# Projections in 64-row pairs, one step of maxima inside every tile, and the maxima turned in the middle of a burst

## The chip, the cores and the metric

The kernel runs on one core of a Trainium2 chip. The metric is device time in microseconds (us) of one launch. The kernel before the change takes 1880.69 us, the median of 3 runs (1880.5 to 1881.56).

A core has a matrix engine (TensorE, in the profile PE, with its weight loads listed apart as PEld), a vector engine (VectorE, DVE), a scalar engine (ScalarE, ACT), a general engine (GpSimd, POOL) and an engine that here only issues transfers (SyncE, SP). Matrix products are written to PSUM, 8 banks of 128 partitions by 512 words; everything else lives in SBUF or in DRAM.

## What is computed

The reference, cut to what matters (S = 2048 rows, D = 640 columns, H = 32 heads of 20):

```python
g = sigmoid((x * gate_w).sum(-1))
qkv = x @ wqkv
scores = einsum("bhqd,bhkd->bhqk", q, k) * 20 ** -0.5
a = softmax(scores) @ v, heads joined, @ wo
re, im = x @ dft_hid_re.T, x @ dft_hid_im.T   # the same x
b = dft_seq_re @ re - dft_seq_im @ im
out = g * a + (1 - g) * b
```

The wqkv and wo inputs are scaled up, so the softmax needs true row maxima, and the kernel splits its matrix operands into two parts (a rounded one and the rest) and adds three products of parts.

## The kernel before

**Stages.** First q, k and v are projected and part of the hidden-dimension DFT is made (to about 255 us of the profile). Then follows the attention, 32 units of one head pair by one half of the rows. Each unit has 32 steps. With it run the rest of the hidden DFT, the sequence DFT and the output projection, as filling work on PE. A short tail writes the last rows.

**Projection stage.** `qk_tile(c, t)` (L302) makes one 128 x 512 tile of q or k: for 5 blocks of D it issues three products of parts (`three`, L118 to L121) into one bank, each with 128 contraction rows, so 15 matmuls. ACT copies the bank into half of a `p` tile (L320), POOL splits the copy into two parts (L115, L116, from `split`), and SP stores it to `qk_scr` (L300, from `flush`). The loop at L438 runs 32 such tiles. Before every third of them `segment` (L378) runs one tile of the hidden DFT. `hid_tile` (L353) works in pairs: every product is cut into two halves of 64 contraction rows, on the upper and lower half of the array, each half with its own bank (`yp0`, `yp1`), 15 pairs of 320 columns; ACT copies one bank and DVE adds the other (L371, L372). Between the pairs `segment` issues four steps of maxima, at the places that FILL gives (0, 8 and 7 pairs apart).

**A step of maxima** (`s_step`, L189, and `s_mm`, L161): two matmuls of 60 contraction rows by 512 columns, one per head of the pair and so one per half of the array, and for each a DVE reduction of the bank to row maxima (L173). These score tiles are made twice: once query-major for the maxima (kind "m" in ORDER), later key-major for the exponential (kind "e", L880, exp on ACT at L886). The maxima run ahead of the exponentials by LEAD = 41 steps. The first 41 are made in the projection stage: 40 in the ten segments, one by `run_s(LEAD)` after the last tile.

**Cycles of the attention.** A cycle is four steps in the order that ORDER writes out: 8 e, 8 m, fillings (F), and at its end B, the burst: `burst(c)` (L892) finishes maxima (`max_nm`, L185), reads out filling work, and runs two `av_step`s (L527): probabilities times values, 128 rows by 21 columns, on four column quarters of the array at a time.

**The turn of the maxima** (`max_chain`, L202). When all 32 steps of a unit have their maxima, `max_nm` reduces them to 128 x 16 (L187). At the end of that burst PE turns the 16 columns into rows (a transpose against `ident`, L205) in a bank of the rotation, DVE splits the result in two parts (16 x 128), and two steps later SP copies them in four transfers (L213, L214) into rows 60 and 61 of each head's block in `qst`. The e-scores have 62 contraction rows: the two extra ones subtract the maxima. So the first e-score of a unit waits for these transfers.

**Banks.** `bank()` (L125) hands out `ps0` to `ps4` in turn; `av`, `yp0` and `yp1` are the other three. SP issues its transfers in program order, and `at_step(i, fn)` places what a function issues at the beginning of step i.

**Weights.** `load_wqk` (L269) is issued after tile t = 1 of a group of four and split there one group later, on ACT and DVE (`fin()`).

Of the kernel before, what the change touches and what calls it, by code (L numbers as in the profile page):

```python
# [11 lines left out]
R = mybir.dt.float32r  # L12
# [28 lines left out]
LEAD = 41  # L41


FILL = {4: (0, 8, 7, 0)}
# [31 lines left out]
def mix_kernel(ctx: ExitStack, tc: tile.TileContext, xa, wqk, wb, cdft, wo, out):  # L76
# [21 lines left out]
    o_scr = dram.tile([D, S], F32, name="o_scr")  # L98

# [23 lines left out]
    turn = itertools.count()  # L123

    def bank():  # L125
        return ps_w.tile([P, 512], F32, name=f"ps{next(turn) % 5}")
# [48 lines left out]
    def s_end(i):  # L175
# [6 lines left out]
        if s == 1 and 0 < n <= NU and now[0] < 0:  # L182
            max_chain(n - 1)

    def max_nm(n):  # L185
        nms[n] = small.tile([P, 16], F32, name="nm", bufs=2)
        dve.tensor_reduce(nms[n], mx.pop(n).rearrange("p h q c -> p (h q) c"), axis=AX.X, op=ALU.max, negate=True)  # L187
# [14 lines left out]
    def max_chain(n):  # L202
        q = q_unit(n)
        pt = bank()[:16, :P]
        pe.transpose(pt, nms.pop(n), ident)  # L205
        m1 = small.tile([16, P], R, name="m1")
        m2 = small.tile([16, P], R, name="m2")
        split(m1, m2, pt, dve, dve)

        def rows():  # L210
            for h in range(2):
                b = 64 * h + KROWS
                sp.dma_start(f32(q[b : b + 1, :]), f32(m1[8 * h : 8 * h + 8, :]))  # L213
                sp.dma_start(f32(q[b + 1 : b + 2, :]), f32(m2[8 * h : 8 * h + 8, :]))  # L214

        if now[0] < 0:
            rows()
        else:
            at_step(now[0] + 2, rows)
# [82 lines left out]
    def qk_tile(c, t):  # L302
        w = wt[c]
# [11 lines left out]
        if hid_done:  # L315
            if not halves:
                raw = pair_tile()
                halves.extend((raw[:, 1], raw[:, 0]))
            raw = halves.pop()
            act.activation(raw, ps, AF.Copy)  # L320
        st = pair_tile()
        st1, st2 = st[:, 0].bitcast(R), st[:, 1].bitcast(R)
        if hid_done:
            split(st1, st2, raw, pool, pool)
        else:
            split(st1, st2, ps, act, dve)
        stores.append((qk_scr[:, t, c * P : (c + 1) * P].rearrange("z p c -> p z c"), st))
        flush(1 if hid_done else 2)
# [24 lines left out]
    def hid_tile(i, read_out):  # L353
        j, st = divmod(i, NS)
        hf, ri = divmod(j, 2)
        new_y(0), new_y(1)
# [21 lines left out]
    def segment(i, steps):  # L378
# [4 lines left out]
        tile_ = hid_tile(i, read_out)  # L383
        for n in FILL[steps]:
            run_s(step + 1)
            for _ in range(n):
                next(tile_)
# [40 lines left out]
    for s in range(0, NS, 2):  # L428
# [6 lines left out]
        if s == 12:  # L435
            fin()
            fin = load_wb(3)
# [606 lines left out]
```

## Time and profile before

| | |
|---|---|
| median of 3 runs | 1880.69 us (1880.5 to 1881.56) |
| the profiled execution's own time | 1881.58 us |
| its span | 1879.7 us |
| DVE busy in the span | 1446.3 us (77%) |
| ACT busy | 1224.5 us (65%) |
| POOL busy | 1075.1 us (57%) |
| granted TensorE clock | 1.00 in nearly every stretch |

Times in the views count from the start of the span. A row of the timeline has the start, the time from the first start to the last end of the merged instructions, the engine, the line, the operation, its tiles and shapes, and their number; in square brackets the idle time of the engine before it and what ended it. Matmuls are pipelined and their ends are modelled, so what a matmul costs is read from the distance between starts, not from its length. The row of a stretch has its length, then for PE, PEld, DVE, ACT and POOL the busy time and the number of instructions, the granted clock, the share of the DMA engines and GB/s.

### The profile page before, as it was taken

The numbers are of one execution on the slowest core, as the hardware profiler recorded it, in microseconds if no ns is written. First come the engines' busy times: TensorE is split into PE (matmuls) and PEld (weight loads), VectorE is DVE, ScalarE is ACT, GpSimd is POOL, SyncE is SP. The second block draws the span as 40 slices with busy tenths as digits, with TensorE's granted clock in tenths as the row PEclk, the third lists the DMA queues.
The fourth block names the chain that finished last, engine by engine and source line by source line (L and its number), as shares of the span: only waits on it lengthen the run. The fifth ranks groups of instructions, "written<-read, shape, count | busy, mean of one in ns | idle before, by whom it ended". The sixth has DMA issues, their size and how long they took to land. (4 is left out here: it accounts for less than half of the span.)

```text
span 1879.7 us, 44556 instructions
## 1 busy us (share of the span) xinstructions
PE 1870.3 (99%) x17453; PEld 1355.1 (72%) x17453; DVE 1446.3 (77%) x2404; ACT 1224.5 (65%) x2359; POOL 1075.1 (57%) x942
## 2 busy tenths in 40 slices
PE   9999999999999999999999999999999999999998
PEld 8988777777776767767677776776767777676666
DVE  4143469989898888888888888888888888889953
ACT  4221147777777767767676676766767667677785
POOL 1234421010045896566799899778789988634334
PEclk9999999999999999999999999999999999999999
DMA  7843341312325473536566576546476746342214
GB/s 233 180 137 141 134 140 48 80 59 66 115 69 185 147 230 125 162 123 189 194 182 226 173 241 197 167 131 188 162 234 197 213 152 202 112 111 68 62 36 159
DMA packets 174597, 280.51 MB, mean 149 GB/s; under 512 B 44095, under 2 KB 106687, under 8 KB 174387
## 3 DMA queue, kind: packets, MB, share of 16 engines
q1 hardware_dynamic: 173427, 275.69, 48.1%
q0 software_dynamic: 960, 1.97, 0.6%
q8 instruction: 137, 2.24, 0.5%
q14 instruction: 73, 0.60, 0.1%
HBM read 213.37 MB, written 63.52 MB: 147 GB/s over the span
## 5 line engine op out<-in xcount | busy, mean ns | idle before, releaser
L173 DVE TENSOR_REDUCE mx<-ps 128x1 f32<-128x512 f32 x2048 | 1296.1, 684 | 219.6 <-PE ps L171 199.6
L886 ACT ACTIVATE p<-ps 128x512 f32<-128x512 f32 x2048 | 1087.9, 598 | 429.3 <-PE ps L171 228.7
L171 PE MATMUL ps<-kst,qst 60*128 60x512 f32 x2048 | 776.5, 413 | 1.5 <-DVE mx L173 1.4
L880 PE MATMUL ps<-qst,kst 62*128 62x512 f32 x2048 | 698.4, 414 | 0.1
L614 PE MATMUL yp<-x,part 64*128 64x320 f32 x5376 | 645.8, 307 | 0.0
L614 PEld LDWEIGHTS yp<-x,part 64*128 64x128 f32 x5376 | 580.7, 186 | 7.2
L533 PE MATMUL av<-p,v 128*21 128x512 f32 x4096 | 490.6, 596 | 0.0
L880 PEld LDWEIGHTS ps<-qst,kst 62*128 62x128 f32 x2048 | 334.8, 184 | 202.5 <-DVE mx L173 182.2
L171 PEld LDWEIGHTS ps<-kst,qst 60*128 60x128 f32 x2048 | 368.2, 184 | 15.0 <-issue 3.8
L116 POOL TENSOR_TENSOR part<-raw,part 128x1024 fp32r<-128x1024 f32 (+1 forms) x129 | 290.3, 2251 | 10.3
L533 PEld LDWEIGHTS av<-p,v 128*21 128x21 f32 x4096 | 98.1, 100 | 225.8 <-issue 225.1
L363 PE MATMUL yp<-wb,x 64*128 64x320 f32 x1920 | 227.7, 307 | 0.3 <-ACT raw L371 0.2
L115 POOL CAST part<-raw 128x1024 fp32r<-128x1024 f32 (+1 forms) x129 | 127.1, 985 | 166.6 <-PE yp L614 155.3
L363 PEld LDWEIGHTS yp<-wb,x 64*128 64x128 f32 x1920 | 202.4, 186 | 5.2 <-DVE raw L372 0.8
L494 POOL TENSOR_TENSOR raw<-raw,raw 128x1024 f32<-128x1024 f32 x77 | 185.5, 2410 | 24.6 <-DMA raw<-in_cdft 23.7
L563 POOL TENSOR_TENSOR o<-o,rb 128x512 f32<-128x512 f32 x31 | 40.2, 1296 | 145.8 <-DMA rb<-r_scr 94.5
L119 PE MATMUL ps<-x,part 128*128 128x512 f32 (+1 forms) x236 | 90.7, 384 | 0.3
L685 PE MATMUL yp<-x,part 64*128 64x320 f32 x720 | 90.9, 310 | 0.0
L121 PE MATMUL ps<-x,part 128*128 128x512 f32 (+1 forms) x236 | 89.6, 380 | 0.1
L120 PE MATMUL ps<-x,part 128*128 128x512 f32 (+1 forms) x236 | 89.1, 377 | 0.0
L116 POOL TENSOR_TENSOR x<-araw,x 128x320 fp32r<-128x320 f32 x96 | 83.8, 873 | 7.7
L320 ACT ACTIVATE p<-ps 128x512 f32<-128x512 f32 x32 | 19.1, 598 | 93.8 <-PE ps L121 93.8
(85 smaller groups left out, 1142.2 us busy)
## 6 DMA issues: line engine op xcount, KB each, us to landing
raw<-in_cdft SPq DMA_DIRECT2D x192, 512.0 KB
araw<-a_scr SPq DMA_DIRECT2D x176, 160.0 KB
qk_scr<-p SPq DMA_DIRECT2D x40, 512.0 KB
kst<-qk_scr SPq DMA_DIRECT2D x90, 160.0 KB
qst<-qk_scr SPq DMA_DIRECT2D x90, 160.0 KB
a_scr<-raw SPq DMA_DIRECT2D x64, 160.0 KB
yt<-y_scr SPq DMA_DIRECT2D x64, 160.0 KB
y_scr<-yt SPq DMA_DIRECT2D x64, 160.0 KB
```

The lines of the kernel that those rows point to most:

```text
L115: e1.tensor_copy(dst1, src)
L116: e2.tensor_tensor(dst2, src, f32(dst1), op=ALU.subtract)
L119: pe.matmul(ps, st1, mv1, start=first, stop=False)
L171: pe.matmul(ps, q[b : b + KROWS, qt * P : (qt + 1) * P], k[b : b + KROWS, kc * 512 : (kc + 1) * 512], start=True, stop=True)
L173: return lambda: dve.tensor_reduce(mx[n][:, h, qt, kc : kc + 1], ps, axis=AX.X, op=ALU.max)
L363: pe.matmul(yp[h][:, :HE], xs[xz][t][r, d, cs], w[r, wz, d, :HE], start=d == 0 and z == 0, stop=d == ND - 1 and z == 2)
L494: pool.tensor_tensor(raws[0], raws[0], raws[1], op=ALU.add if PRODUCTS[n][0][1][0] > 0 else ALU.subtract)
L533: pe.matmul(av[32 * j : 32 * j + DH + 1, :], v[:, kt, h * (DH + 1) : (h + 1) * (DH + 1)], pp[qc][:, h, :], start=kt == 0, stop=kt == NS - 1)
L614: pe.matmul(yp[h][:, :HE], c[r, cz, cs], a[r, az], start=s == 0 and z == 0, stop=s == NS - 1 and z == 2)
L685: pe.matmul(yp[h][:, :HE], o[r, oz, d], wos[d, hf][r, wz], start=d == 0 and z == 0, stop=d == ND - 2 and z == 2)
L880: pe.matmul(pt, k[b : b + KROWS + 2, kt * P : (kt + 1) * P], q[b : b + KROWS + 2, qc * 512 : (qc + 1) * 512], start=True, stop=True)
L886: act.activation(pts[n, kt, qc][:, h], pt, AF.Exp, scale=float(DH) ** -0.5)
```

## The change

LEAD goes from 41 to 43. The projection tiles of the loop at L438 are made as the hidden DFT's are: each of the 15 products is a pair of 64-row matmuls into two banks, `ps0`/`ps1` and `yp0`/`yp1` by turns; ACT copies one bank, DVE adds the other, POOL splits as before. One step of maxima is issued after the seventh pair of every tile, hidden DFT or projection: 42 in 42 tiles, one more behind the last. While this stage runs, the maxima rotate through `ps2` to `ps4` only.

The turn of the maxima moves from the end of the burst in which they are finished to the middle of the next one, between its two `av_step`s. It is no longer one transpose but four plain matmuls, one for each quarter of 32 columns of `ident`, with the 16 columns of maxima doubled to 32, so that each fills one of the four column quarters of the array; the result is 128 x 32. DVE splits that, SP stores both parts to DRAM (`m_scr`, one transfer) one step later, and two steps after that loads them back from there into the rows of `qst` (four transfers, in pieces of 32 words).

```diff
--- before.py
+++ after.py
@@ -38,10 +38,10 @@
 FIRST = {"e": (0, 0, 1, 1), "m": (1, 1, 1, 1)}
 
 
-LEAD = 41
-
-
-FILL = {4: (0, 8, 7, 0)}
+LEAD = 43
+
+
+MARKS = (7,)
 HEAD = 10
 
 
@@ -96,6 +96,7 @@
     r_scr = dram.tile([NU, 4, 512], F32, name="r_scr")
     l_scr = dram.tile([NU, 4, 512], F32, name="l_scr")
     o_scr = dram.tile([D, S], F32, name="o_scr")
+    m_scr = dram.tile([NU, P, 2, 32], F32, name="m_scr")
 
     ident = const.tile([P, P], F32, name="ident")
     make_identity(nc, ident)
@@ -120,10 +121,15 @@
         pe.matmul(ps, st1, mv2, start=False, stop=False)
         pe.matmul(ps, st2, mv1, start=False, stop=last)
 
-    turn = itertools.count()
+    turn, twos, free = itertools.count(), itertools.count(), [range(5)]
 
     def bank():
-        return ps_w.tile([P, 512], F32, name=f"ps{next(turn) % 5}")
+        return ps_w.tile([P, 512], F32, name=f"ps{free[0][next(turn) % len(free[0])]}")
+
+    def two_banks():
+        if next(twos) % 2:
+            return [ps_w.tile([P, 512], F32, name=f"ps{z}") for z in range(2)]
+        return [ps_y.tile([P, 512], F32, name=f"yp{z}") for z in range(2)]
 
     def pair_tile():
         return work.tile([P, 2, 512], F32, name="p", bufs=5)
@@ -180,11 +186,12 @@
             else:
                 ends.append(n)
         if s == 1 and 0 < n <= NU and now[0] < 0:
-            max_chain(n - 1)
+            turn_max(n - 1)
 
     def max_nm(n):
-        nms[n] = small.tile([P, 16], F32, name="nm", bufs=2)
-        dve.tensor_reduce(nms[n], mx.pop(n).rearrange("p h q c -> p (h q) c"), axis=AX.X, op=ALU.max, negate=True)
+        nms[n] = small.tile([P, 32], F32, name="nm", bufs=2)
+        m = mx.pop(n).rearrange("p h q (o c) -> p o (h q) c", o=1).to_broadcast([P, 2, 16, 4])
+        dve.tensor_reduce(nms[n].rearrange("p (o k) -> p o k", o=2), m, axis=AX.X, op=ALU.max, negate=True)
 
     def s_step(i):
         for fn in [s_mm(i, h) for h in range(2)]:
@@ -199,24 +206,32 @@
         return yp[z]
 
 
-    def max_chain(n):
+    def turn_max(n):
         q = q_unit(n)
-        pt = bank()[:16, :P]
-        pe.transpose(pt, nms.pop(n), ident)
-        m1 = small.tile([16, P], R, name="m1")
-        m2 = small.tile([16, P], R, name="m2")
-        split(m1, m2, pt, dve, dve)
-
-        def rows():
+        pt = bank()[:, :32]
+        nm = nms.pop(n)
+        for j in range(4):
+            c = slice(32 * j, 32 * j + 32)
+            pe.matmul(pt[c, :], nm, ident[:, c], start=True, stop=True)
+        m = small.tile([P, 2, 32], R, name="m")
+        split(m[:, 0], m[:, 1], pt, dve, dve)
+
+        def store():
+            sp.dma_start(m_scr[n], f32(m))
+
+        def load():
             for h in range(2):
-                b = 64 * h + KROWS
-                sp.dma_start(f32(q[b : b + 1, :]), f32(m1[8 * h : 8 * h + 8, :]))
-                sp.dma_start(f32(q[b + 1 : b + 2, :]), f32(m2[8 * h : 8 * h + 8, :]))
+                for z in range(2):
+                    b = 64 * h + KROWS + z
+                    sp.dma_start(f32(q[b : b + 1, :]).rearrange("o (k j c) -> o k j c", j=4, c=32),
+                                 m_scr[n, :, z].rearrange("(o j k) c -> o k j c", o=1, j=4)[:, 8 * h : 8 * h + 8])
 
         if now[0] < 0:
-            rows()
+            store()
+            load()
         else:
-            at_step(now[0] + 2, rows)
+            at_step(now[0] + 1, store)
+            at_step(now[0] + 3, load)
 
 
     pa = pools(name="att", bufs=1)
@@ -300,6 +315,8 @@
             sp.dma_start(*stores.pop(0))
 
     def qk_tile(c, t):
+        if hid_done:
+            return qk_pairs(c, t)
         w = wt[c]
         ps = bank()
         x1, x2 = xs[0][t], xs[1][t]
@@ -312,20 +329,36 @@
                 pe.matmul(ps, w[:, 0, d], x2[:, d], start=False, stop=d == ND - 1)
             else:
                 three(ps, w[:, 0, d], w[:, 1, d], x1[:, d], x2[:, d], d == 0, d == ND - 1)
-        if hid_done:
-            if not halves:
-                raw = pair_tile()
-                halves.extend((raw[:, 1], raw[:, 0]))
-            raw = halves.pop()
-            act.activation(raw, ps, AF.Copy)
         st = pair_tile()
-        st1, st2 = st[:, 0].bitcast(R), st[:, 1].bitcast(R)
-        if hid_done:
-            split(st1, st2, raw, pool, pool)
-        else:
-            split(st1, st2, ps, act, dve)
+        split(st[:, 0].bitcast(R), st[:, 1].bitcast(R), ps, act, dve)
+        store_qk(c, t, st, 2)
+
+    def store_qk(c, t, st, keep):
         stores.append((qk_scr[:, t, c * P : (c + 1) * P].rearrange("z p c -> p z c"), st))
-        flush(1 if hid_done else 2)
+        flush(keep)
+
+    def tick(pairs):
+        if pairs in MARKS:
+            run_s(min(step + 1, LEAD))
+
+    def qk_pairs(c, t):
+        w = wt[c]
+        ps = two_banks()
+        for d in range(ND):
+            for z, (wz, xz) in enumerate(((0, 0), (0, 1), (1, 0))):
+                for h in range(2):
+                    r = slice(64 * h, 64 * h + 64)
+                    pe.matmul(ps[h], w[r, wz, d], xs[xz][t][r, d], start=d == 0 and z == 0, stop=d == ND - 1 and z == 2)
+                tick(3 * d + z + 1)
+        if not halves:
+            raw = pair_tile()
+            halves.extend((raw[:, 1], raw[:, 0]))
+        raw = halves.pop()
+        act.activation(raw, ps[0], AF.Copy)
+        dve.tensor_tensor(raw, raw, ps[1], op=ALU.add)
+        st = pair_tile()
+        split(st[:, 0].bitcast(R), st[:, 1].bitcast(R), raw, pool, pool)
+        store_qk(c, t, st, 1)
 
     def mm_b(j, s, ps, n):
         w = wt["b", j]
@@ -353,7 +386,7 @@
     def hid_tile(i, read_out):
         j, st = divmod(i, NS)
         hf, ri = divmod(j, 2)
-        new_y(0), new_y(1)
+        yp[:] = two_banks() if i < HEAD else [new_y(0), new_y(1)]
         w = wt["b", 2 + j]
         t, cs = st // 4, slice(st % 4 * P, (st % 4 + 1) * P)
         for d in range(ND):
@@ -375,16 +408,13 @@
         yield
 
 
-    def segment(i, steps):
+    def hid_first(i):
         def read_out(read, args):
             read()
             stores.append(args)
 
-        tile_ = hid_tile(i, read_out)
-        for n in FILL[steps]:
-            run_s(step + 1)
-            for _ in range(n):
-                next(tile_)
+        for pairs, _ in enumerate(hid_tile(i, read_out)):
+            tick(pairs + 1)
 
     step = 0
 
@@ -435,11 +465,12 @@
         if s == 12:
             fin()
             fin = load_wb(3)
+    free[0] = range(2, 5)
     for n, c in enumerate(order):
         for t in range(4):
             m = 4 * n + t
             if m % 3 == 0 and hid_done < HEAD:
-                segment(hid_done, 4)
+                hid_first(hid_done)
                 hid_done += 1
             qk_tile(c, t)
             if m == 8:
@@ -449,6 +480,7 @@
                     fin()
                 if n + 2 < len(order):
                     fin = load_wqk(order[n + 2])
+    free[0] = range(5)
     run_s(LEAD)
     flush()
 
@@ -889,16 +921,20 @@
 
             held.append(exp) if hold else exp()
 
+    turned = []
+
     def burst(c):
         for n in ends:
             max_nm(n)
         run_extras(max(done - HIDS, 0) // 3, 2)
         for kt in (2 * c, 2 * c + 1):
             av_step(now[0], kt // NS, kt % NS)
+            while turned:
+                turn_max(turned.pop(0))
             while held:
                 held.pop(0)()
-        while ends:
-            max_chain(ends.pop(0))
+        turned[:] = ends
+        ends.clear()
         if c == HID - 1:
             start_dft()
 
```

## The prediction

> **What bounds the kernel now.** I read the page first, then stretches of the span, then the order of time on single engines.
>
> ```profile
> PE 1870.3 (99%) x17453; PEld 1355.1 (72%) x17453; DVE 1446.3 (77%) x2404; ACT 1224.5 (65%) x2359; POOL 1075.1 (57%) x942
> L173 DVE TENSOR_REDUCE mx<-ps 128x1 f32<-128x512 f32 x2048 | 1296.1, 684 | 219.6 <-PE ps L171 199.6
> ```
>
> PE has work for the whole span, so whatever shortens the time must take something out of PE's stream: instructions, or gaps between their starts. DVE is the next engine (77%), nearly all of it reductions of maxima at 684 ns.
>
> The stretches: the projection stage, the first cycle of the attention, a cycle without and one with a turn of maxima, a late cycle with all 8 maxima and the last one that has any (4).
>
> ```profile
> 105.88:254.60 148.72, 147.20 (x862) 119.23 (x861) 60.99 (x101) 28.69 (x51) 62.63 (x62) 1.00 0.38 136
> 254.60:261.43 6.83, 6.65 (x54) 4.99 (x53) 6.29 (x11) 5.05 (x9) 1.90 (x2) 1.00 0.60 192
> 286.38:292.67 6.29, 6.29 (x64) 4.48 (x62) 5.56 (x10) 4.57 (x9) 0.00 (x0) 1.00 0.07 26
> 292.67:299.10 6.43, 6.43 (x65) 4.48 (x63) 6.12 (x13) 4.57 (x9) 0.00 (x0) 1.00 0.15 34
> 1790.12:1796.20 6.08, 6.08 (x58) 4.05 (x56) 5.54 (x10) 4.63 (x9) 3.23 (x4) 1.00 0.00 0
> 1802.38:1807.77 5.39, 5.39 (x53) 3.52 (x52) 4.63 (x10) 4.43 (x9) 3.09 (x4) 1.00 0.00 0
> ```
>
> In the projection stage DVE is busy 61 of 148.7 us, ACT 29, POOL 63: only PE can set its length. In a cycle DVE has 5.56 of 6.29 us: PE sets it, with some 0.7 us of room.
>
> PE in the projection stage, one segment, the five tiles behind it, and the two segments that stall:
>
> ```profile
> 233.88 0.73 PE L171 MATMUL ps<-kst,qst 60*128 60x512 f32 x4
> 234.44 1.34 PE L363 MATMUL yp<-wb,x 64*128 64x320 f32 x16
> 235.62 0.40 PE L171 MATMUL ps<-kst,qst 60*128 60x512 f32 x2
> 235.86 1.19 PE L363 MATMUL yp<-wb,x 64*128 64x320 f32 x14
> 236.89 0.40 PE L171 MATMUL ps<-kst,qst 60*128 60x512 f32 x2
> 237.22 0.50 PE L119 MATMUL ps<-x,part 128*128 128x512 f32 x1
> ...
> 254.28 0.40 PE L121 MATMUL ps<-x,part 128*128 128x512 f32 x1
> 254.60 0.50 PE L171 MATMUL ps<-kst,qst 60*128 60x512 f32 x2
> ```
>
> ```profile
> 133.79 0.72 PE L171 MATMUL ps<-kst,qst 60*128 60x512 f32 x4
> ...
> 136.63 0.50 PE L171 MATMUL ps<-kst,qst 60*128 60x512 f32 x1 [0.70 <-DVE mx L173]
> ...
> 138.43 0.50 PE L119 MATMUL ps<-x,part 128*128 128x512 f32 x1
> ```
>
> ```profile
> 193.36 0.50 PE L171 MATMUL ps<-kst,qst 60*128 60x512 f32 x1 [0.70 <-DVE mx L173]
> ```
>
> ```profile
> 135.15 0.82 DVE L116 TENSOR_TENSOR part<-raw,part 128x640 fp32r<-128x640 f32 x1 [9.14 <-ACT part L113]
> ```
>
> The 75 matmuls from 237.22 to 254.28 are 17.06 / 74 = 0.2305 us apart. Every change between 128-row and 64-row matmuls shows as a longer step: 0.32 instead of 0.23 at 254.28, 0.33 instead of 0.24 at 236.89. A plain segment takes 237.22 - 233.88 = 3.34 us; the one at 133.79 takes 4.64. There, four steps of maxima stand within 3 us, DVE came to them late because its queue held a split of weights (135.15), the banks were not free, and PE waited. The same happens at 193.36.
>
> **Pairs in the projections.** A pair does the work of one 128-row matmul, with twice the instructions. Its price is not in the trace for 512-wide projections, but its neighbours are: a step of maxima is a 512-wide pair, 0.24 us (235.62 to 235.86), and a 320-wide pair with the same 128-column weights takes 1.18 / 8 = 0.1475, so two weight loads fit even there. Lower bound the stream itself, 0.2305; upper bound 0.24. I take 0.2305: inside a run of pairs nothing changes width, and the matmul streams the same 512 columns.
>
> The stage after: 32 x 15 x 0.2305 = 110.6, 150 hidden pairs x 0.1475 = 22.1, 43 steps x 0.24 = 10.3 (two more than before), 0.1 for entering it and 0.3 for the first unit's turn: 143.4 against 148.72, **5.3 us less**. By parts that is ten times two changes of tile (about 0.2 us each time), the two stalls of 1.3, and less the two added steps (0.5). At 0.24 a pair the gain is 5.3 - 480 x 0.0095 = 0.7.
>
> What must stay hidden there: each tile adds a DVE addition, for which the nearest row is
>
> ```profile
> L116 DVE TENSOR_TENSOR p<-ps,p 128x512 fp32r<-128x512 f32 x8 | 5.3, 687 | 17.7 <-ACT p L113 17.7
> ```
>
> 0.69 us. With two reductions (1.37) DVE has 2.1 us of work in a tile of 15 x 0.2305 + 0.24 = 3.7 us, PE being the cover; POOL starts 0.7 later and has its slack in the first stretch above. A tile's banks are asked for again two tiles later, 3.7 us after its last matmul, against 0.6 + 0.69 us of read-out. Steps come 3.7 us apart on three banks, so the split of weights that stalled two segments delays two reductions and no longer PE. Cover gone (DVE late by more than a tile): 1.3 us each time, as seen.
>
> **The seam to the attention** loses. DVE sets the first cycle:
>
> ```profile
> 254.71 0.60 ACT L320 ACTIVATE p<-ps 128x512 f32<-128x512 f32 x1 [2.76 <-PE ps L121]
> ```
>
> ```profile
> 255.14 7.44 DVE L173 TENSOR_REDUCE mx<-ps 128x1 f32<-128x512 f32 x12 [15.46 <-PE ps L171]
> ```
>
> 6.29 of 6.83 us busy, twelve reductions without a gap, and PE waiting on banks. After the change the last tile's addition stands ahead of them in DVE's queue: ACT's copy ends 1.03 after the last matmul starts, the addition 0.69 later, so the reductions start at 1.72 instead of 255.14 - 254.28 = 0.86: **0.9 us more**. Bounds: 0 if later slack in DVE takes it up, 2 if the last `p` tiles, which POOL now finishes later, are waited for too.
>
> **The turn of the maxima.** PE and its weight loads in two bursts:
>
> ```profile
> 286.38 1.91 PE L533 MATMUL av<-p,v 128*21 128x512 f32 x16
> 288.23 0.50 PE L880 MATMUL ps<-qst,kst 62*128 62x512 f32 x1
> ```
>
> ```profile
> 292.67 1.92 PE L533 MATMUL av<-p,v 128*21 128x512 f32 x16
> 294.52 0.28 PE L205 MATMUL ps<-ident,nm 128*16 128x128 f32 x1
> 294.73 0.49 PE L880 MATMUL ps<-qst,kst 62*128 62x512 f32 x1
> ```
>
> ```profile
> 292.67 0.14 PEld L533 LDWEIGHTS av<-p,v 128*21 128x21 f32 x8 [0.24 <-issue]
> 293.12 0.12 PEld L533 LDWEIGHTS av<-p,v 128*21 128x21 f32 x4 [0.31 <-issue]
> 293.55 0.12 PEld L533 LDWEIGHTS av<-p,v 128*21 128x21 f32 x4 [0.31 <-issue]
> ```
>
> ```profile
> L205 PE MATMUL ps<-ident,nm x32: 276/277/278, 220.3 to 1809.6; 128*16 128x128 f32 x32
> ```
>
> The transpose makes the way from burst to next score 2.06 instead of 1.85 us: 0.21 each, in 31 bursts (the first turn is in the projections). In the middle of the burst the quarters use the array as the `av` products around them do: 128 rows, one column quarter each, four at a time. The rows show an fp32 product as two passes (16 records for two `av_step`s of 4), and a pass of 512 columns on four quarters takes 293.55 - 293.12 = 0.43 us. Two passes of 32 columns: 2 x 0.43 / 16 = 0.05. The weights of a pass of 128 columns in all load in the shadow of the pass ahead, except the second set, whose pass ahead is this short one; eight loads in 0.14 us put that at 0.02 or less. I take 0.07, a gain of 0.14 x 31 = **4.2 us**. Bounds: 0.05 (4.8 us), and, if PE drained ahead of and behind the quarters (0.1 each, as at the changes of tile above), 0.28, a loss of 2.2 us.
>
> The Trainium skill (TensorE: Matmul & The Clock Gate, Back-to-back issue gap) speaks against this part: however small its width, a matmul does not start sooner than about 25 ns after the one before. Eight such starts would by an estimate from that page take 0.2 us. The trace's weight loads, eight in 0.14 us, do not bear that out for neighbouring quarters.
>
> DVE's part stays about as it is (two splits of 0.28 at 16 x 128 now; smaller at 128 x 32; the reduction ahead of them reads twice as much), and falls into the burst, when DVE has its room. The turn uses one bank as before. SP gets five issues for four, one of which waits for another.
>
> **LEAD 43.** The two added steps are counted above. They fall out of the end: the cycle at 1802.38 loses its last 4 maxima. From 8 to 4 a cycle went from 6.08 to 5.39, 0.17 each; ACT has 4.43 us in it, so there is room: **0.5 us less** of the 0.69. The end of a unit's maxima moves one cycle forward, which leaves the turn in the cycle in which it is now.
>
> **Sum:** 5.3 - 0.9 + 4.2 + 0.5 = 9.1 us. The span would be 1879.7 - 9.1 = 1870.6; the profiled execution ran 1881.58, 0.05% above the median, so the same 9.1 come off the median: 1880.69 - 9.1 = **1871.6**.
>
> **Rivals.**
>
> *The rows of maxima come late (slower).* They now go by DRAM, and every unit's first e-scores wait for them.
>
> ```profile
> 295.14 0.66 SPq L213 DMA_DIRECT2D qst<-m  x1
> ...
> 297.27 0.64 SPq L214 DMA_DIRECT2D qst<-m  x1
> ```
>
> ```profile
> 304.97 0.46 PE L880 MATMUL ps<-qst,kst 62*128 62x512 f32 x2
> ```
>
> ```profile
> SPq L550 <- DMA l_scr<-o: 12.4, 12, 2.8
> ```
>
> ```profile
> 1819.20 1.28 POOL L563 TENSOR_TENSOR o<-o,rb 128x512 f32<-128x512 f32 x1 [0.86 <-DMA rb<-r_scr]
> ```
>
> ```profile
> 1813.93 1.75 SPq L560 DMA_DIRECT2D rb<-r_scr  x4
> ```
>
> From turn to need there are 304.97 - 294.52 = 10.45 us, and 0.86 more as the turn is two passes earlier. The chain at upper prices: 0.62 to the first issue, the store's issue 0.66 and its landing 2.8 (the longest wait of a load for a small store), four issues 297.91 - 295.14 = 2.8, a landing of 1819.20 - 1815.68 = 3.5: 10.4 of 11.3. Hidden by 0.9. It decides from there on: if SP's queue held store or loads 2 us longer (another transfer's wait between them), 30 units would each lose 1.1, 33 us, and the time be 1871.6 + 33 = 1905. For it: program order on SP, behind both. Against it: today's first issue follows the turn by 0.62.
>
> *The quarters cost what the transpose did*, by drains or by a floor on starts: 1871.6 + 4.2 = 1875.8.
>
> *512-wide pairs run at 0.24*, as a step of maxima between narrower pairs does: 1871.6 + 4.6 = 1876.2.
>
> *Both*, or one with the longer seam: about 1880, no change.
>
> **How the numbers follow.** Forecast (1869 to 1874) 0.60; quarters as dear as now 0.15; slow pairs 0.10; both, no change 0.07; rows late 0.08. From these, **1871.6**; the range 1867.5 to 1879 leaves out the late rows, most of the no-change case and a little below. A difference of 0.2% (3.8 us, about what a measurement of this kernel can tell from none) is 1876.9: faster 0.82, same 0.10, slower 0.08.
>
> **What would show it.** Pairs: projection matmuls of 64 rows 0.23 us apart, no step longer than 0.24 around the maxima, a stage of 143 us. Turn: burst starts to next score about 1.92 us in the cycle of a turn. Seam: the first reductions of the attention start 0.9 later. Rows: no wait of L880's weights for `qst` at the first score of a unit. Wrong it would be made by pairs over 0.24, by a wait there, or by a PE wait on banks in the projections.

## The result, and the profile after

The changed kernel takes 1871.3 us (median of 4, 1870.43 to 1871.84), the kernel before in the same session 1881.12 (median of 4): a ratio of 0.9947 with a 95% interval of 0.9935 to 0.9959. It is 9.8 us faster by the medians and 10.3 by the spans (1879.7 to 1869.4). The forecast was 1871.6.

The page of the kernel after, the busy time of the engines, the groups of the maxima and of the new projection pairs, and the queue of program fetches:

```profile
PE 1859.3 (99%) x18157; PEld 1356.1 (73%) x18157; DVE 1468.8 (79%) x2436; ACT 1223.4 (65%) x2359; POOL 1077.1 (58%) x942
...
q8 instruction: 143, 2.34, 0.5%
...
L179 DVE TENSOR_REDUCE mx<-ps 128x1 f32<-128x512 f32 x2048 | 1297.9, 684 | 200.0 <-PE ps L177 179.7
...
L351 PE MATMUL ps<-x,part 64*128 64x512 f32 x630 | 84.0, 390 | 0.0
```

PE still has work for the whole span, with more instructions than before; DVE has 22 us more, the additions of the pairs. ACT and POOL stay within 2 us of what they were. The stretches that answer to those of before: projection stage, first cycle, all cycles up to the last burst, tail.

```profile
105.90:249.79 143.89, 143.30 (x1353) 122.88 (x1354) 87.19 (x136) 28.71 (x51) 63.21 (x62) 1.00 0.39 141
249.79:257.33 7.54, 7.03 (x54) 4.88 (x50) 6.71 (x11) 4.96 (x9) 1.89 (x2) 1.00 0.53 172
257.33:1840.60 1583.27, 1583.27 (x16005) 1113.77 (x16004) 1331.27 (x2228) 1142.50 (x2203) 977.73 (x828) 1.00 0.50 147
1840.60:1869.40 28.80, 21.79 (x139) 18.46 (x138) 15.97 (x29) 9.52 (x18) 12.50 (x14) 0.95 0.53 197
```

The stage fell from 148.72 to 143.89 us, the first cycle rose from 6.83 to 7.54.

**The pairs.** PE in three projection tiles of the stage after:

```profile
235.08 1.77 PE L351 MATMUL yp<-x,part 64*128 64x512 f32 x14
236.68 0.41 PE L177 MATMUL ps<-kst,qst 60*128 60x512 f32 x2
236.92 2.01 PE L351 MATMUL yp<-x,part 64*128 64x512 f32 x16
238.76 1.77 PE L351 MATMUL ps<-x,part 64*128 64x512 f32 x14
240.36 0.40 PE L177 MATMUL ps<-kst,qst 60*128 60x512 f32 x2
```

Seven pairs take 240.36 - 238.76 = 1.60 us, eight take 238.76 - 236.92 = 1.84: 0.23 each, as forecast. The step of maxima between them takes 0.24. No distance between starts is longer here. Both stalls of before, 1.3 us each, are gone. One of 0.75 us has come up at another place, in the second hidden tile; PE, then DVE at the same place:

```profile
120.52 0.39 PE L177 MATMUL ps<-kst,qst 60*128 60x512 f32 x1
121.50 0.49 PE L177 MATMUL ps<-kst,qst 60*128 60x512 f32 x1 [0.59 <-DVE mx L179]
```

```profile
117.53 3.32 DVE L117 TENSOR_TENSOR wb<-raw,wb 128x966 fp32r<-128x966 f32 x2 [0.21 <-ACT wb L114]
120.77 1.27 DVE L179 TENSOR_REDUCE mx<-ps 128x1 f32<-128x512 f32 x2
```

The two halves of a weight block, split on DVE, last 3.3 us, nearly a whole tile (3.68 us, from 235.08 to 238.76), and hold up the reductions that free a bank. The kernel before made the same split at the same place, without a stall; there the maxima had five banks, not three:

```profile
117.94 2.88 DVE L116 TENSOR_TENSOR wb<-raw,wb 128x966 fp32r<-128x966 f32 x2 [6.26 <-ACT wb L113]
```

**The turn.** A burst with its turn, PE and then the weight loads:

```profile
288.49 1.06 PE L565 MATMUL av<-p,v 128*21 128x512 f32 x8
289.36 0.24 PE L215 MATMUL ps<-ident,nm 128*32 128x32 f32 x8
289.42 1.04 PE L565 MATMUL av<-p,v 128*21 128x512 f32 x8
290.39 0.50 PE L912 MATMUL ps<-qst,kst 62*128 62x512 f32 x1
```

```profile
288.93 0.13 PEld L215 LDWEIGHTS ps<-ident,nm 128*32 128x32 f32 x4 [0.31 <-DVE mx L179]
289.36 0.13 PEld L215 LDWEIGHTS ps<-ident,nm 128*32 128x32 f32 x4 [0.30 <-issue]
289.39 0.15 PEld L565 LDWEIGHTS av<-p,v 128*21 128x21 f32 x8
```

The eight records of the four quarters (two passes) take 289.42 - 289.36 = 0.06 us, and the `av` products ahead of them and behind them go on as if nothing stood between. Their weights load while the products before are still running (288.93); the load of the transpose, which started at 294.52 in the burst shown before, came only when its own turn had come:

```profile
294.51 0.09 PEld L205 LDWEIGHTS ps<-ident,nm 128*16 128x16 f32 x1 [0.85 <-DVE nm L187]
```

From burst to next score it is 290.39 - 288.49 = 1.90 us where it was 2.06.

**Where the 10.3 us come from.** Stage to its last projection matmul -4.7, from there to the first burst +0.6, from burst 0 to burst 244 -7.1, from 244 to 246 (the last maxima) -1.0, from the last burst to the end **+1.9**. The last was in no sum.

**The tail.** DMA in GB/s, in 40 slices of the time from the last burst to the end, before and after, and the SP issues of the last eight stores:

```profile
GB/s 365 15 0 0 0 0 0 259 228 0 0 255 339 381 400 354 241 61 65 61 61 388 423 176 0 148 385 419 415 183 396 362 358 366 411 419 404 122 0 0
```

```profile
GB/s 316 14 29 0 0 0 36 391 29 0 139 356 388 388 352 213 43 57 57 192 384 384 7 18 384 377 398 231 393 352 96 85 395 402 377 391 203 18 0 0
```

```profile
1869.84 6.13 SPq L954 DMA_DIRECT2D out_y<-x  x8
```

```profile
1857.64 7.05 SPq L990 DMA_DIRECT2D out_y<-x  x8
```

After, transfers fall to a quarter in the 31st and 32nd slice (96 and 85 GB/s, 21.6 to 23.0 us behind the last burst); before, the lowest slice in that part has 183. One of SP's eight issues, begun 20.96 us behind the last burst, took 1431 ns instead of 332. DVE finished its last rows 22.65 us behind the last burst in both: the work wasn't late, its stores were.

### The profile page after: what moved, and what is told of

It reads as the page before. It is cut to its first block, busy times and chain, and to the rows that moved or that the text cites. A ratio compares the mean times of both kernels' runs of the same rounds, so it can differ in the third digit from the quotient of the medians.

```text
span 1869.4 us, 46025 instructions
## 1 busy us (share of the span) xinstructions
PE 1859.3 (99%) x18157; PEld 1356.1 (73%) x18157; DVE 1468.8 (79%) x2436; ACT 1223.4 (65%) x2359; POOL 1077.1 (58%) x942
## 3 DMA queue, kind: packets, MB, share of 16 engines
q8 instruction: 143, 2.34, 0.5%
## 5 line engine op out<-in xcount | busy, mean ns | idle before, releaser
L918 ACT ACTIVATE p<-ps 128x512 f32<-128x512 f32 x2048 | 1087.0, 599 | 423.8 <-PE ps L177 217.0
L646 PEld LDWEIGHTS yp<-x,part 64*128 64x128 f32 x5376 | 580.5, 186 | 7.5
L177 PEld LDWEIGHTS ps<-kst,qst 60*128 60x128 f32 x2048 | 372.7, 184 | 11.0 <-DVE mx L179 1.4
L117 POOL TENSOR_TENSOR part<-raw,part 128x1024 fp32r<-128x1024 f32 (+1 forms) x129 | 290.6, 2253 | 10.3
L351 PE MATMUL ps<-x,part 64*128 64x512 f32 x630 | 84.0, 390 | 0.0
L717 PEld LDWEIGHTS yp<-x,part 64*128 64x128 f32 x720 | 77.7, 186 | 2.9
L351 PEld LDWEIGHTS ps<-x,part 64*128 64x128 f32 x630 | 65.4, 185 | 11.3
L734 POOL TENSOR_TENSOR x<-x,m 128x320 f32<-128x320 f32 x30 | 26.2, 873 | 80.1 <-DVE m L729 63.9
```

Source lines behind the costliest of these rows:

```text
L117: e2.tensor_tensor(dst2, src, f32(dst1), op=ALU.subtract)
L177: pe.matmul(ps, q[b : b + KROWS, qt * P : (qt + 1) * P], k[b : b + KROWS, kc * 512 : (kc + 1) * 512], start=True, stop=True)
L351: pe.matmul(ps[h], w[r, wz, d], xs[xz][t][r, d], start=d == 0 and z == 0, stop=d == ND - 1 and z == 2)
L646: pe.matmul(yp[h][:, :HE], c[r, cz, cs], a[r, az], start=s == 0 and z == 0, stop=s == NS - 1 and z == 2)
L717: pe.matmul(yp[h][:, :HE], o[r, oz, d], wos[d, hf][r, wz], start=d == 0 and z == 0, stop=d == ND - 2 and z == 2)
L918: act.activation(pts[n, kt, qc][:, h], pt, AF.Exp, scale=float(DH) ** -0.5)
```

## The experiments

All spans and parts of the path in one table, to be read with each experiment. "Start" is where the projection stage begins, "stage" goes from there to its last projection matmul, "seam" to the first burst of the attention; 244 to 246 are the last two cycles with maxima; the tail begins at the last burst. Between 246 and the last burst lie 39.5 us in all but e5 (44.4).

| kernel | span | start | stage | seam | bursts 0 to 244 | 244 to 246 | tail |
|---|---|---|---|---|---|---|---|
| before | 1879.7 | 105.9 | 148.39 | 7.15 | 1540.96 | 10.86 | 26.95 |
| after | 1869.4 | 105.9 | 143.67 | 7.76 | 1533.90 | 9.85 | 28.83 |
| e1 turn only | 1874.3 | 106.1 | 148.48 | 9.38 | 1533.88 | 9.84 | 27.06 |
| e2 pairs only | 1876.0 | 106.1 | 143.43 | 7.80 | 1540.47 | 10.87 | 27.84 |
| e3 transpose mid-burst | 1878.9 | 105.8 | 143.66 | 7.90 | 1543.74 | 10.08 | 28.15 |
| e4 quarters at the end | 1870.3 | 106.6 | 143.67 | 7.76 | 1533.63 | 10.04 | 29.06 |
| e5 lead 41 | 1968.6 | 106.5 | 143.43 | 7.65 | 1628.20 | 10.38 | 28.05 |
| e6 128-row tiles | 1883.6 | 107.6 | 159.10 | 6.98 | 1533.57 | 9.84 | 27.05 |
| e7 last step early | 1870.3 | 106.0 | 143.90 | 7.08 | 1535.52 | 9.85 | 28.47 |
| e8 and the split on POOL | 1867.5 | 105.8 | 142.88 | 7.08 | 1534.62 | 9.84 | 27.74 |
| e9 after, 78 more PE instructions ahead | 1874.5 | 112.9 | 143.67 | 7.77 | 1533.75 | 9.84 | 27.06 |
| e10 e8, likewise | 1874.5 | 112.1 | 142.88 | 7.07 | 1534.82 | 9.84 | 28.29 |
| e11 after again | 1869.5 | 106.7 | 143.65 | 7.76 | 1533.74 | 9.86 | 28.31 |
| e12 two tiles first | 1869.7 | 113.1 | 137.13 | 7.44 | 1535.57 | 9.85 | 27.07 |

**e1: the turn and the lead alone.** The projections stay as they were; LEAD, `max_nm`, `turn_max` and `burst` are those of the change.

```diff
-LEAD = 41
+LEAD = 43
...
-    def max_chain(n):
+    def turn_max(n):
```

> The new turn of the maxima with LEAD 43, on the projection stage of before (128-row tiles, four steps in each segment, three steps behind the last tile). Theory (the parts add up, and the turn is worth 0.147 us in each of 31 bursts): bursts with a turn reach the next score after 1.91 us instead of 2.05, their cycles are 0.14 to 0.15 us shorter than before, the two late cycles around the last maxima together 1.0 us shorter; the projection stage keeps its 148.7 us and grows by the two added steps (0.5 us); the first cycle is 1 to 2.5 us longer, as DVE has four more reductions ahead of it. Span 1876 to 1878. Rival (the turn gains only because the projections changed the state in which the attention starts): cycles with a turn as long as before, 6.44 to 6.51 us.

1876.07 us against 1881.63. The stage stays at 148.5, and the cycles are those of the change: 1533.88 from burst 0 to 244. The seam takes 9.38: without a place inside the tiles the two added steps stand behind the last tile. The span of 1874.3 us lies below the 1876 expected, as the cycles without a turn came out shorter too; point by point below.

**e2: the pairs alone.** LEAD 41 and the turn as it was, the projections of the change.

```diff
-LEAD = 43
+LEAD = 41
...
-    def turn_max(n):
+    def max_chain(n):
```

> The projections in pairs with a step in every tile, with LEAD 41 and the old turn by a transpose at the end of the burst. Theory: projection stage 143.4 us (143.9 less two steps), first cycle 0.7 us longer than before, every cycle with a turn as before (2.05 us from burst to next score), late cycles as before: span 1879.7 - 5.3 + 0.7 = 1875. Rival (the gain of the stage needs the two further steps, or the attention gains from the new start): cycles shorter by more than 0.02 us on the median, or a stage over 145 us.

1877.83 us. The stage takes 143.43, the cycles are those of before. So the two parts lie side by side: by spans e1 gains 5.5 us, e2 3.7, together 9.2 of the 10.3. Without the tails, which are taken up at e9 to e11, it is 5.5 and 4.6 of 12.2; LEAD's two steps are free only where both are in (e1 pays 2.2 for them in its seam).

**e3: the transpose, moved into the middle of the burst.** The place of the change with the old operation.

```diff
-        for j in range(4):
-            c = slice(32 * j, 32 * j + 32)
-            pe.matmul(pt[c, :], nm, ident[:, c], start=True, stop=True)
+        pe.transpose(pt, nms.pop(n), ident)
```

> As after the change, but the turn is the old single transpose (128 columns moving, 16 stationary) with the old four transfers from SBUF; it stands in the middle of the next burst, as the quarters do. Theory A (the width that is streamed pays: 128 columns on one quarter against 2 x 32 on four at once): 0.12 us or more of the 0.21 us stays. Theory B (the drain at the change from scores to transpose paid, and the middle of the burst avoids it): burst to next score falls to 1.91 us or below, as with quarters.

1880.64 us, and dearer than either theory had it. PE in the same burst:

```profile
288.55 1.06 PE L555 MATMUL av<-p,v 128*21 128x512 f32 x8
289.54 0.28 PE L210 MATMUL ps<-ident,nm 128*16 128x128 f32 x1
289.74 1.06 PE L555 MATMUL av<-p,v 128*21 128x512 f32 x8
290.73 0.49 PE L902 MATMUL ps<-qst,kst 62*128 62x512 f32 x1
```

The way from burst to score is 2.18 us. Ahead of the transpose PE loses 289.54 - 288.55 - 0.87 = 0.12, the 0.87 being what the same eight products took in the kernel after (288.49 to 289.36); the transpose itself takes 0.20. At the end of the burst some 0.10 are paid anyway, at the step to the scores: the eight products from 289.42 to 290.39 in the kernel after take 0.97. The Trainium skill (TensorEngine Tiling (Array Packing), Key Properties) says that changing the tiling mode, and not just the tile, drains TensorE. The 0.12 us fit that, but the row doesn't name the mode in which the transpose runs.

**e4: the quarters, at the end of the burst.** The operation of the change in the old place.

```diff
-            while turned:
-                turn_max(turned.pop(0))
             while held:
                 held.pop(0)()
+        while turned:
+            turn_max(turned.pop(0))
```

> As after the change, but the quarters stand at the end of the next burst, behind both attention steps, instead of between them. Theory A (width pays): burst to next score stays at about 1.91 us. Theory B (the place pays): it rises to 2.0 or more, as PE then drains once more before the scores of 64 rows. DVE's two splits now fall behind the burst, 0.4 us, which theory A expects to cost under 0.05 us a cycle.

1872.16 us. From burst to score 1.906 us in the cycles of a turn, the same as in the middle:

```profile
289.18 1.91 PE L565 MATMUL av<-p,v 128*21 128x512 f32 x16
290.91 0.24 PE L215 MATMUL ps<-ident,nm 128*32 128x32 f32 x8
291.08 0.50 PE L912 MATMUL ps<-qst,kst 62*128 62x512 f32 x1
```

So it is the operation that counts, not the place: four quarters follow `av` without a loss wherever they stand in the burst. With e3, all four corners are measured: transpose 0.21 at the end and 0.34 in the middle, quarters 0.06 at both. What makes the transpose dear, its form on the array or its weights that load late, no run takes apart.

**e5: LEAD 41 with all the rest.** The rows then have one cycle less.

```diff
-LEAD = 43
+LEAD = 41
```

> As after the change, but with LEAD 41, which puts the turn one cycle (6.3 us) later against the first score that needs its rows. After the change the way from turn to first score is 11.3 us, and in its trace the last of the four loads is issued 5.3 to 6 us after the turn and takes 0.64 us to issue. Theory (typical prices: a landing of about 1.5 us, rows there some 7.5 to 8 us after the turn): with 5.0 us left each of 31 units waits about 2.5 to 3 us at its first score, span 1869.4 + 31 x 2.8 = about 1955. Rival (the upper prices of the prediction, 10.4 us): 5.4 us a unit, about 2035. If nothing changes by more than 5 us, the chain is shorter than 5 us and never was a danger.

1970.35 us, 99 more. SP and PE of the turn at 350.12:

```profile
351.69 0.38 SPq L220 DMA_DIRECT2D m_scr<-m  x1
353.24 2.75 SPq L226 DMA_DIRECT2D qst<-m_scr  x4
```

```profile
350.12 0.24 PE L215 MATMUL ps<-ident,nm 128*32 128x32 f32 x8
...
357.51 0.61 PE L912 MATMUL ps<-qst,kst 62*128 62x512 f32 x2 [2.20 <-DMA qst<-m_scr]
358.06 3.54 PE L565 MATMUL av<-p,v 128*21 128x512 f32 x16
```

The wait that the late-rows rival spoke of is there, and it gives the chain's length: 357.51 - 350.12 = 7.4 us here. Over the units it is 6.3 to 9.6, in the median 7.2 (5.0 in the last unit, whose cycles are shorter), and 2.0 to 3.4 of it lie behind the start of the last issue. About 3.2 us are lost in each of 31 units, in all 14 more than expected. The waits make 60 of the 99 us. Most of the rest is clock: at or just behind 15 of the 31 waits the clock that was granted falls to half, for 3.4 us and three times for 6.8, together 61 us, worth up to 30. The burst behind the wait shown takes 3.54 us for that reason, where 1.91 is usual:

```profile
357.96:361.37 3.41, 3.41 (x18) 0.52 (x16) 0.49 (x1) 1.42 (x3) 0.00 (x0) 0.50 0.14 49
```

The rows of the transfers in the kernel after:

```profile
290.97 0.38 SPq L220 DMA_DIRECT2D m_scr<-m  x1
...
293.19 3.19 SPq L226 DMA_DIRECT2D qst<-m_scr  x4
```

```profile
300.65 0.47 PE L912 MATMUL ps<-qst,kst 62*128 62x512 f32 x2
```

From the turn at 289.36 to the need at 300.65 there are 11.3 us. By e5's lengths some 4 are to spare as a rule, and 1.7 in the worst unit.

**e6: the projections in 128-row matmuls again, with the steps inside the tiles.** The stage then changes between forms of the array twice at every step.

```diff
-                for h in range(2):
-                    r = slice(64 * h, 64 * h + 64)
-                    pe.matmul(ps[h], w[r, wz, d], xs[xz][t][r, d], ...)
+                pe.matmul(ps[0], w[:, wz, d], xs[xz][t][:, d], ...)
...
-        dve.tensor_tensor(raw, raw, ps[1], op=ALU.add)
```

> As after the change, but the projection tiles are made of 15 matmuls of 128 rows into one bank again (no DVE addition), with the step of maxima inside each tile; hidden tiles in pairs as they are. Theory (each change between 128-row and 64-row matmuls costs 0.1 to 0.2 us): two changes for the step in each of 32 tiles and two for each of the 10 hidden tiles, 84 in all: stage longer by 84 x 0.1 to 84 x 0.2, 8 to 17 us; the first cycle of the attention 0.7 us shorter, as the addition is gone. Rival (the gain of the stage came from the spreading of the steps, not from the pairs): stage within 3 us of 143.7.

1885.43 us, the stage 159.10: 15.4 us more for 84 changes, 0.18 each.

```profile
239.75 1.54 PE L349 MATMUL ps<-x,part 128*128 128x512 f32 x6
241.21 0.49 PE L177 MATMUL ps<-kst,qst 60*128 60x512 f32 x2
241.64 2.13 PE L349 MATMUL ps<-x,part 128*128 128x512 f32 x8
243.70 1.29 PE L393 MATMUL yp<-wb,x 64*128 64x320 f32 x14
```

A step takes 0.43 us here and 0.24 among pairs. The six matmuls ahead of it take 1.46, where six without a change take 6 x 0.229 = 1.37, and the eight behind it 2.06, where eight take 1.83; 0.10 of these lies at their end, at the change to the hidden tile, and 0.11 at the second of them. So going from 128 to 64 rows costs 0.10 us and coming back 0.30. The pairs are worth having only because everything in the stage then uses the array in one way; the matmuls themselves cost the same.

**e7: the 43rd step early**, in the tile m = 12, so that none stands behind the last tile.

```diff
                 hid_first(hid_done)
+                if m == 12:
+                    run_s(step + 1)
```

> As after the change, but the 43rd step of maxima stands behind the hidden tile ahead of tile 12 instead of behind the last tile, so that only the last tile's addition is ahead of the attention's reductions in DVE's queue. Theory (DVE's order of work sets the first cycle): the seam from the last projection matmul to the first burst is 1.3 us shorter (two reductions), about 6.5 us; the stage grows by 0.24; net 1.0 less. Rival (the last p tiles, which POOL finishes later, set it): seam unchanged but for the 0.24 us of PE.

1872.12 us: no gain. The seam falls by 0.68, half of what was expected, the stage rises by 0.23, and the cycles take 1.6 us more: 0.3 of it in the very first and 1.2 in one long cycle (number 147).

**e8: e7, and the split of the last weight block on POOL** instead of ACT and DVE.

```diff
-            fin = load_wb(3)
+            fin = load_wb(3, pool, pool)
```

> As the run before (43rd step early), and the split of the fourth block of B weights, which is first needed by the seventeenth hidden tile, goes from ACT and DVE to POOL. Theory (the one stall left in the stage, 0.75 us at the second hidden tile, comes from DVE's split of these weights ahead of two reductions): stage 0.75 us shorter, no stall there. Rival (POOL's split of about 5 us delays the projections' own splits until the p tiles run out): another stall of more than 0.5 us behind it.

1869.39 us in its one run. The stage takes 142.88, 1.0 less than in e7. The first cycle, 6.84 us instead of 6.23, takes back most of what the seam gained. The stall is gone:

```profile
120.44 0.42 PE L177 MATMUL ps<-kst,qst 60*128 60x512 f32 x2
120.68 1.35 PE L396 MATMUL yp<-wb,x 64*128 64x320 f32 x16
```

**e9 to e11: what the tail hangs on.** PE's program comes in blocks by DMA (queue q8 of the page: 143 fetches of 16 KB). e9 is the kernel after with 78 more PE instructions in its opening, so that these blocks end elsewhere; e10 is e8 with the same; e11 is the kernel after itself, once more.

```diff
-    idle(8)
+    idle(3, 44)
...
+        for _ in range(short):
+            pe.matmul(ps[:, :64], zeros[:, :P], zeros[:, :64], start=True, stop=True)
```

> As after the change, but of the 8 idle matmuls that open PE's stream 5 are replaced by 44 short ones (64 columns), 39 matmuls and 39 weight loads more, while PE waits for the first inputs. It moves the point at which PE's next 16 KB of program are fetched by 78 instructions, in the tail some 5.7 us earlier: from 20.4 to about 14.6 us behind the start of the last burst. Theory (a program fetch among the last output stores holds up one of the transfer engines): from the last burst to the end 27.0 us as in the kernels whose fetch fell at 11 to 16 us, against 28.8 after the change; everything between as it was; time 1.8 us less, 1869.5. Rival (the longer tail comes from elsewhere, and the fetch only stands near it): tail still 28.5 or more.

> The three mends together: 43rd step early, the fourth B block split on POOL, and the opening with 78 instructions more on PE. Theory (parts add): stage to the last projection 142.9 us, seam 7.1, attention as after the change, tail 27.0: span 1866 to 1868, time 1868 to 1869.5, faster than the changed kernel by 2 to 3 us. Rival (single cycles that are hit by 0.1 to 0.9 us, at other places in each program, are as large as these gains): no difference to 1871.3 beyond the spread.

> The changed kernel once more, for a second trace. If single long cycles of the attention and the tail belong to the program (to where its fetches fall), they stand at the same cycles again (9, 80, 147, 204, 215) with a tail of 28.8 us; if they are chance, at others.

e9: 1876.3 us (median of 7, ratio to before 0.9973, 0.9962 to 0.9983). Its fetch came 12.4 us behind the last burst, 8 us earlier (5.7 were expected), and its tail did what was expected, 27.06 us. But its opening cost 7 us: the short matmuls, meant as idle work, take 9.60 / 44 = 0.22 us each.

```profile
1.46 9.60 PE L280 MATMUL ps<-x 128*128 128x64 f32 x44 [1.46 <-DVE x L274]
```

```profile
GB/s 254 4 12 0 0 0 0 265 220 0 0 262 357 376 383 360 208 58 85 61 83 383 398 167 0 174 395 387 402 231 349 391 364 364 387 402 383 140 0 0
```

The hole at the 31st and 32nd slice has gone. e10: 1875.25 (median of 6, ratio 0.9968, 0.9956 to 0.9980), with the same loss in the opening, and a tail of 28.29, although its fetch came early, at 12.2 us: DVE ended 1.2 us later. What came late is the last of four loads, which took 1507 ns to issue instead of 707, begun while the fetch ran; ACT's split of the loaded block starts 1.75 us later. The four loads in e10, then in e9, where a fetch at nearly the same place left them alone:

```profile
1856.25 3.90 SPq L1019 DMA_DIRECT2D raw<-o  x4
```

```profile
1857.52 3.10 SPq L1017 DMA_DIRECT2D raw<-o  x4
```

e11: 1871.32, again a long tail, 28.31, with the fetch at the same place.

**e12: the program shorter instead of longer.** e8 with the first two tiles in 128-row matmuls ahead of the first hidden tile, 60 PE instructions fewer.

```diff
-            if m % 3 == 0 and hid_done < HEAD:
+            if m % 3 == 2 and hid_done < HEAD:
...
-                if m == 12:
+                if m in (14, 20, 26):
```

> The changed kernel with the fourth B block split on POOL, the first two projection tiles of the stage made as 128-row tiles ahead of the first hidden tile (the v products in front of them have 128 rows too, so no change of tile is added), and the three steps that these two tiles and the end give up placed behind hidden tiles 5, 7 and 9. PE's program is 60 instructions shorter than in the run with the seam and the B block mended; its last program fetch came 27 instructions ahead of PE's end, so it should not come at all. Theory (fetch among the last stores costs 0.7 to 2.1 us): from the last burst to the end 27.0 us, against 27.7 to 28.8; seam 7.1, stage with its two first tiles no longer than 142.9; time 1868 to 1869, 2 to 3 us below the changed kernel's 1871.3. Rival (the fetch moves, but is not lost, or the steps behind the hidden tiles stall): tail 28 or more, or a stage over 144.

1870.76 us (median of 5, ratio 0.9946, 0.9932 to 0.9959). The tail is 27.07; the late fetch is gone from it, and the one ahead of that falls at 4.15 us. The stage counts from its first hidden tile, so the two tiles ahead of it lie in the start. With them it takes 144.1 us, where at most 142.9 were expected, the seam takes 7.44 for 7.1, and the cycles take 1.7 us more than those of the kernel after. Its interval is that of the change: a version that beats the changed kernel isn't shown. e8 had the lowest time, in one run.

The start of the one program fetch in the tail, from the packets of each trace, in us behind the last burst, with the tail:

```
e12   e1    before  e9    e6    | e3    e2    e8    e7    e11   e5    after e4    | e10
4.15  15.3  11.4    12.4  16.1  | 18.3  18.4  20.0  20.1  20.3  20.3  20.35 21.3  | 12.2
27.07 27.06 26.95   27.06 27.05 | 28.15 27.84 27.74 28.47 28.31 28.05 28.83 29.06 | 28.29
```

## Why the prediction was right, point by point

**The bound** held: PE set the time of the stage and of the cycles, and what came out of its stream came off the time.

**Pairs in the projections**: forecast 0.2305 us a pair, measured 0.23; the rival of 0.24 fell. The stage gained 4.8 us, not 5.3: that a split of weights "delays two reductions and no longer PE" was half right. It holds for the two splits that stalled PE before. A third, longer one (2.9 us, at 117.94 before), which the prediction doesn't weigh, now stalls PE for 0.75 us; this is the PE wait on banks that the prediction named as a sign against it. e8 shows whose it is: with that split off DVE the stall is gone and the stage 1.0 shorter. That the gain lies in the changes of tile stands on e6 (0.18 each). The prediction's check by parts doesn't come out, though: with 0.2 us for each segment's two changes it makes 4.1 us, and with 0.2 for each change 6.1. By the starts in the trace before, a segment's two changes cost 0.30: 0.10 ahead of it, 0.09 behind it, and 0.11 more at the second matmul after that (0.34 instead of 0.23), which the mean of 0.2305 hides.

**The seam**: forecast 0.9, measured 0.6 to 0.7. The mechanism is the one named, the last tile's addition ahead of the reductions:

```profile
250.62 0.69 DVE L358 TENSOR_TENSOR p<-p,ps 128x512 f32<-128x512 f32 x1 [1.18 <-ACT p L357]
251.22 7.42 DVE L179 TENSOR_REDUCE mx<-ps 128x1 f32<-128x512 f32 x12
```

The reductions start 251.22 - 249.57 = 1.65 us behind the start of the last projection matmul, 0.8 more than before. e6, which leaves the addition out, has a seam 0.78 shorter.

**The turn**: forecast 0.07 a turn, measured 0.061 (1.906 against 1.845 us in the cycles without one), against 0.207 before: 0.146 x 31 = 4.5, forecast 4.2. That quarters stand among `av` products without a loss was right; the place in the middle of the burst gains nothing (e4). The bound that priced drains "ahead of and behind" belongs to the transpose (e3), not to quarters. The Trainium skill (TensorE: Matmul & The Clock Gate, Back-to-back issue gap) gives about 25 ns as the least time between two starts. The eight passes here take 0.06 us, under 8 ns a start: across neighbouring column quarters the measurement doesn't bear the floor out.

**LEAD 43**: forecast 0.5, measured 1.0 less from burst 244 to 246: 0.58 in the one cycle that loses its last maxima, which is the term as forecast, and 0.43 in the next, 0.15 of it the turn in that cycle's burst.

**Rows late**: didn't happen. The upper price of 10.4 of 11.3 us left 0.9; e5 puts the chain at 6.3 to 9.6, so 10.4 was high for most units and close for the worst. The last landing was taken too high: 3.5 us were borrowed from another transfer, and in e5 the rows were there 1.3 to 2.8 us behind the end of the last issue. The threshold, though, is real, and e5 is what lies behind it: two steps of lead less cost 99 us.

**What wasn't in the sum.** The tail, +1.9. And 7.1 us came out of bursts 0 to 244, where 30 turns at 0.146 make 4.4. The other 2.6 lie in cycles without a turn: the 214 of them went from 6.300 to 6.288 us (median), and one of 7.15 us is ordinary now. The lower median comes with the quarters, in e1, e4 and e6 as in the change, and not with the pairs (e2) or the transpose in the middle (e3). Why is open. The long cycles are the same ones when the same program runs again (numbers 9, 80, 147, 204 and 215 in the kernel after and in e11), so they aren't chance. They are the same in e4, and in e9 too, where PE's fetches fall 78 instructions elsewhere, so these fetches don't explain them; in e1, e2 and e3 most are others. The sum of 9.1 was close to the 9.8 since these two misses, +1.9 and -2.6, and the smaller ones nearly cancel: that the number came out so near is luck, while the terms for pairs, seam and turn were right for their reasons.

## What to carry to other kernels

Price a small PE operation by what stands beside it: if it uses the array in the same form as its neighbours, it costs its columns (0.06 us here); if not, each change of form comes on top (0.10 us one way and 0.30 the other between 128 and 64 rows in e6, 0.12 ahead of the transpose in e3). Rewriting work so that a whole stage has one form can be worth doubling its instructions. A chain through DRAM is checked by taking its lead away until it shows: that one run gives its length unit by unit, and so the margin of the worst one.

## What the hardware showed that wasn't expected

**A program fetch can delay the last stores.** Where the 16 KB fetch came 16.1 us or less behind the last burst, the tail took 26.95 to 27.07 us in five kernels; where it came 18.3 us or more behind, among the last stores, it took 27.7 to 29.1 in eight. e9 moves the fetch by 8 us and leaves the rest of the program behind the opening as it was: 28.83 us (28.31 in e11) become 27.06. e10 stands outside this rule, with an early fetch beside a load that came late. In the kernel after, the issue of 1431 ns begins while the fetch runs (20.35 to 22.02), and the whole trace is like that: from 120 us on, of SP's 97 issues that begin during a fetch 25 take over 0.4 us longer than is usual on their line, and of the 1144 with no fetch within a microsecond 5. Over all fourteen traces it is 327 of 1262 and 80 of 16112. The Trainium skill (Runtime: NRT & Kernel Launch, Instruction fetch mechanics) says that an engine fetches its program in blocks of 16 KiB, 256 instructions, on a DMA queue of its own, and that the cost of a block's end is mostly hidden. The 143 fetches agree with the size (2.34 MB, and 2 x 18157 matmuls and weight loads make 254 instructions a fetch); in the tail the cost isn't hidden, up to 2.1 us. By what means a fetch of PE's program holds up SP's issues isn't shown.

**Short matmuls at the start of a program aren't cheap.** 64 columns with 128-column weights took 0.22 us each in e9's opening. The eight of 512 columns in the opening of the kernel after are slow too: the matmul behind them starts at 5.11, so they take (5.11 - 1.46) / 8 = 0.46 each, where one takes 0.23 in the projection stage. So an eighth of the columns still costs half the time:

```profile
1.46 3.78 PE L280 MATMUL ps<-x 128*128 128x512 f32 x8 [1.46 <-DVE x L274]
```

**A wait can cost more than its length.** Of e5's 31 waits the 11 of up to 1.12 us leave the granted clock at 1.00; of the 20 longer ones (1.3 to 4.3 us) 15 have it at half, at or behind their end, for 3.4 us or more. What decides among the longer ones isn't shown.
